# Chunked attention and two expert layers on one core: unread products placed by the planner, two weight loads under way, v in whole groups

## The chip, the cores and the metric

One core of a Trainium2 chip runs one program. The metric is the device time in microseconds (us) of one execution. TensorE is called PE, VectorE DVE, ScalarE ACT, GpSimd POOL, and SyncE SP; SP issues the DMA transfers.

## The reference

```python
for c in range(768 // 32):                     # chunks of 32 queries, 4 batches, 8 heads, 64 wide
    q_c = q[:, :, 32*c : 32*c + 32]
    keys = concat(mem_k, k[32*c - 16 : 32*c + 40])   # 8 memory keys, 16 to the left, 8 to the right
    a = softmax(q_c @ keys.T / 8)
    out[chunk] = a @ concat(mem_v, v[the same])
x = out as (3072 tokens, 512)
h = x @ w_in            # 512 x 2048
x = (h * clip(h + 3, 0, 6) / 6) @ w_out        # 2048 x 512
h = x @ moe2_w_in
y = max(0.01 * h, h) @ moe2_w_out
```

## The kernel before

The host only lays data out: q, k and v are cut into groups of 96 tokens and come as `raw`; the four weight matrices come as 64-bit numbers whose two halves the kernel joins to float32 (`decode`: one ACT instruction, L397, and four of DVE, L400, L404, L408 and L412). Every float32 operand of the layers is split into a high and a low part of type fp32r (a copy on ACT, L342, and a subtraction on DVE, L345), and a product of layers is three fp32r products: high with high, low with high, high with low.

The work on PE is the two layers, in blocks of 512 tokens; the attention is put between their products. The first block of tokens needs four pieces of attention before its first product: two units of 384 tokens (`unit`, one for each half of the heads; PSUM tiles `at` and `ab`) and two half units of 192 tokens (`half_unit` with `gp` 0, tiles `h` and `ac`). Then come two more half units (`gp` 1, tile `at`) and the units of the other tokens. A piece goes: scores on PE (L549, L816), maximum on DVE, exp on ACT (L573, L585, L842, L850), sum and norm on DVE (L603, L867), transposes on PE (L607, L871), a copy to SBUF on ACT (`take_p`), the product with v on PE (L627, L639, L887, L899), and the result into the operands `xh` (ACT) and `xl` (DVE). In front of the scores the keys are copied into windows (`windows`, on ACT, DVE or POOL).

The loads of v come in two layouts. "Whole" groups (`gp` 0: `whole = not gp`) take 128 rows per transfer, 4 transfers, and POOL copies the memory rows to their places (`memory`). The half units with `gp` 1 take 8 transfers instead, four of 56 partitions (L790) and four of 8 partitions (L792).

The order of all this is set by `schedule`. Each piece of work is a `Task` with a function that emits its instructions, a duration per engine, a key (its due place) and the buffers that it takes and uses. `schedule` simulates the five engines by these durations, the DMA queue by rates (`RATE...`) and constants, and the supply of PE's instructions by `feed` (`HELD`, `FETCHED`, `FETCH`), and at each free moment emits the task with the lowest key that is ready. The engines then run in exactly that order, each held only by semaphores. A task that was planned too early holds everything behind it on its engine.

Some products on PE are read by nobody: the identity with itself, written into a PSUM bank (`warm`, L466). The call `warm(n, after, home)` puts n of them behind a named task, by hand: 512 columns each into `ac` before and between the scores, 256 columns each into `ac` later on.

```python
    warm(2)
    warm(1, marks["s", 0, 0])
    warm(2, marks["s", 0, 1])
    warm(1, marks["s", 1, 0, 0])
    home = marks["b", 1, 1, 0][0]
    for m, n in ((("s", 1, 1, 0), 2), (("t", 0, 0), 3), (("t", 0, 1), 3), (("t", 1, 1, 0), 2), (("v", 1, 0, 0), 2)):
        warm(n, marks[m], home)
```

Of the kernel before, what the change touches and what calls it, by code (L numbers as in the profile page):

```python
# [23 lines left out]
QK = 2 * G + 2 * KW  # L24
# [33 lines left out]
RATE_QK, RATE, RATE_V, COLD = 380.0, 220.0, 300.0, 1.1  # L58
# [10 lines left out]
class Task:  # L69


    def __init__(self, fn, opts, key, after=(), allocs=(), uses=(), moe=False, issues=1, late=0, loads=False, ins=8):
        self.late, self.loads, self.ins = late, loads, ins
# [21 lines left out]
STARTS, LANDS, SURE = 1900.0, 500.0, 1500.0  # L95
HELD, FETCHED, FETCH, STALL = 447, 256, 5000.0, 250.0
# [7 lines left out]
def schedule(tasks, places, ends):  # L104
# [10 lines left out]
    queue = (0, HELD, None)  # L115
# [43 lines left out]
    def finish(task, e):  # L159
        for b in task.bufs:  # L160
# [17 lines left out]
    while events:  # L178
# [10 lines left out]
        while again:  # L189
            again = False  # L190
            for e, h in heaps.items():
# [44 lines left out]
                if e == "SP" or pick.loads:  # L236
                    at = now
                    for _ in range(pick.issues):
                        at = max(at, lanes[e].pop(0)) + ISSUE[e]
                        wire = max(wire, at + STARTS) + d / pick.issues  # L240
                        lanes[e].append(wire + LANDS)
                    free[e] = at if pick.loads else max(at, wire - QUEUED)
                    push(free[e], "free", None)
                    push(wire + LANDS + (SURE if pick.allocs else 0.0), "done", (pick, e))
# [12 lines left out]
def tile_attn_moe_moe2(ctx: ExitStack, tc: tile.TileContext, raw, w1i, w1o, w2i, w2o, out):  # L257
# [131 lines left out]
    def decode(src, f, key, early=None, after=(), place="wm", gate=(), late=0, own=True, split=None):  # L389
# [3 lines left out]
        def load(e):  # L393
            nc.sync.dma_start(out=make(t, ([128, 512, 2], U32)).rearrange("p w s -> p (w s)"), in_=src[f])
# [19 lines left out]
        k = add(load, {"SP": dma(524288, 380.0)}, key - 30 if early is None else early, after=after, allocs=[t])  # L414
# [31 lines left out]
    xbuf, xdone, turn, sent = {}, {}, [], {}  # L446

# [9 lines left out]
    marks = {}  # L457

    def warm(n, after=None, home=None):

        b, c = home or Buf("ac"), 2 if home else 4

        def fn(e):
            x = made(b)[:, 1, N - 128 * c:].rearrange("p (a n) -> p a n", a=c)
            for _ in range(n):
                nc.tensor.matmul(x, ident, ident.unsqueeze(1).to_broadcast([128, c, 128]), start=True, stop=True, skip_group_check=True)  # L466

        add(fn, {"PE": c * n * (220.0 if after else 430.0)}, after.key + 0.5 if after else -200.0, after=[after] if after else [], allocs=[] if home else [b], uses=[home] if home else [], ins=4 * n)

    def unit(j, quad, key, tag, own=False, direct=False, loads=None):  # L470
# [254 lines left out]
        t = marks["s", j, quad] = add(scores, {"PE": (COLD if direct else 1.0) * 1300.0}, key - 16, ins=192, after=t, allocs=[ps], uses=[*qk, *kw])  # L725
        scored = t
        if direct and quad in SHIFT:
            t = add(greatest, {"DVE": 2100.0}, key - 15, after=[t], allocs=[mx, e], uses=[ps])
            t = add(exp_all, {"ACT": act(2 * PAIRS * W)}, key - 13, after=[t], uses=[e])
            t = add(total, {"DVE": 1250.0}, key - 12, after=[t], allocs=[s], uses=[e])  # L730
        else:
# [4 lines left out]
            t = add(exp(1), {"ACT": 6 * 330.0}, key - 13, after=[t], uses=[ps, mx, e, s])  # L736
            t = add(total, {"DVE": 350.0}, key - 12, after=[t], uses=[s])
        t = add(norm, {"DVE": 900.0} if direct else {"POOL": 1800.0, "DVE": 900.0}, key - 11, after=[t], uses=[e, s])
        t = marks["t", j, quad] = add(transpose, {"PE": (COLD if direct else 1.0) * 600.0}, key - 7, ins=12, after=[t], uses=[e, ps])
        t = add(take_p, {"ACT": act(PAIRS * 128)}, key - 5, after=[t], uses=[pt, e])  # L740
# [950 lines left out]
```

## Time and profile before

| | |
|---|---|
| median of 3 runs (lowest, highest) | 1047.82 us (1047.02, 1048.76) |
| profiled execution | 1049.14 us, of which the span of instructions is 1047.40 |
| mean granted TensorE clock in it | 0.992 of full speed |
| PE busy | 1035.1 us, 99% of the span |
| DVE, ACT, POOL busy | 875.3, 693.7, 20.8 us |
| DMA | 220.49 MB, mean 211 GB/s |
| first product of the layers | 39.77 us after the span's start |

The profile's own time is that of a single execution; the median of the runs stands 1.32 us below it. Busy time of PE says that an instruction was in its pipeline, not that the array ran at full rate. A line such as L345 is that of a helper, so the tile names tell which work it is: `x4` counts records, and a float32 product on PE leaves two matmul records and two weight loads, a transpose one of each.

### The profile page before, as it was taken

The page shows a single profiled execution, that of the slowest core. Times are in us where ns is not written, and L with a number is a line of the kernel's source. Part 1 is how long each engine was busy: PE and PEld are TensorE (multiplying, and loading weights), DVE is VectorE, ACT ScalarE, POOL GpSimd, SP SyncE. Part 2 cuts the span into 40 slices and gives each one's busy share as a digit, 9 for nine tenths or more (in the row PEclk, how much of TensorE's full clock was granted, in tenths as well). Part 3 has the DMA queues.
Part 4 walks back from the last instruction along what each step waited for, and adds up shares of the span by engine and source line. Part 5 has one row for each costly group of instructions (what it writes and reads, how often), then busy time and mean ns, then how long its engine had stood idle before and what let it go on. Part 6 is the DMA issues. An engine that isn't in the chain of part 4 may idle for free.

```text
span 1047.4 us, 20225 instructions
## 1 busy us (share of the span) xinstructions
PE 1035.1 (99%) x7476; PEld 850.3 (81%) x7476; DVE 875.3 (84%) x1485; ACT 693.7 (66%) x1480; POOL 20.8 (2%) x30
## 2 busy tenths in 40 slices
PE   7999999999999999999999999999999999999998
PEld 4778988888788888888888888888888888888886
DVE  6898988778998778799999899999576998566775
ACT  4786876655888555476686576785565874666753
POOL 3010000000000000000000000000000000000000
PEclk8899999999999999999999999999999999999999
DMA  9889787876887979673648778546342454423451
GB/s 265 283 216 331 241 291 230 258 229 221 262 282 239 332 225 290 239 239 123 214 144 268 253 251 280 183 158 221 111 171 81 174 193 156 173 109 96 146 181 61
DMA packets 127314, 220.49 MB, mean 211 GB/s; under 512 B 12528, under 2 KB 76016, under 8 KB 127216
## 3 DMA queue, kind: packets, MB, share of 16 engines
q1 hardware_dynamic: 127216, 219.20, 63.9%
q8 instruction: 59, 0.97, 0.4%
q14 instruction: 39, 0.32, 0.1%
HBM read 156.24 MB, written 62.91 MB: 209 GB/s over the span
## 4 chain that ended last, share of the span: by engine, by line
PE 89%; DVE 4%; DMA 3%; ACT 3%; issue 1%; SPq 0%; DVEq 0%; ACTq 0%
PE y L1327 15%; PE y L1052 13%; PE y L1495 12%; PE h L1327 10%; PE h L1495 8%; PE hx L1495 8%; PE h L1003 7%; PE hx L1327 7%; PE h L1052 2%; PE at L639 2%; DMA w<-in_raw 2%; PE at L549 1%; DVE w L345 1%; PE at L607 1%; PE ac L466 1%
## 5 line engine op out<-in xcount | busy, mean ns | idle before, releaser
L345 DVE TENSOR_TENSOR w<-w 128x512 fp32r<-128x512 f32 (+2 forms) x393 | 322.9, 854 | 25.8 <-ACT w L342 23.9
L342 ACT CAST w<-w 128x512 fp32r<-128x512 f32 (+1 forms) x290 | 223.3, 803 | 13.4 <-PE hx L1495 3.6
L1052 PE MATMUL y<-g,w 128*128 128x512 f32 (+1 forms) x540 | 125.2, 375 | 0.9 <-ACT g L342 0.7
L1327 PE MATMUL y<-w 128*128 128x512 f32 x516 | 124.6, 390 | 0.0
L1327 PEld LDWEIGHTS y<-w 128*128 128x128 f32 x516 | 96.6, 188 | 20.1
L1052 PEld LDWEIGHTS y<-g,w 128*128 128x128 f32 x540 | 94.1, 189 | 19.0 <-ACT g L342 1.2
L342 ACT CAST g<-w 128x512 fp32r<-128x512 f32 x80 | 49.4, 620 | 63.8 <-PE y L1495 23.0
L1495 PE MATMUL y<-w 128*128 128x512 f32 x384 | 90.3, 389 | 0.0
L1495 PEld LDWEIGHTS y<-w 128*128 128x128 f32 x384 | 72.1, 188 | 14.9
L1301 ACT ACTIVATE w<-w 128x512 f32<-128x512 f32 x72 | 45.0, 630 | 40.4 <-DVE w L1372 18.1
L1003 PE MATMUL h<-xh,w 128*128 128x512 f32 (+1 forms) x288 | 66.1, 370 | 0.5 <-DVE w L345 0.5
L345 DVE TENSOR_TENSOR g<-w,g 128x512 fp32r<-128x512 f32 x80 | 54.1, 684 | 14.3 <-ACT g L342 14.2
L1495 PE MATMUL h<-w 128*128 128x512 f32 x264 | 62.1, 389 | 0.0
L1495 PE MATMUL hx<-w 128*128 128x512 f32 x252 | 59.2, 389 | 0.0
L1327 PE MATMUL h<-xl,w 128*128 128x512 f32 x240 | 58.3, 391 | 0.0
L1495 PEld LDWEIGHTS h<-w 128*128 128x128 f32 x264 | 49.6, 188 | 10.3
L1003 PEld LDWEIGHTS h<-xh,w 128*128 128x128 f32 x288 | 49.7, 189 | 9.9 <-DVE w L345 0.9
L1495 PEld LDWEIGHTS hx<-w 128*128 128x128 f32 x252 | 47.3, 188 | 9.8
L1327 PEld LDWEIGHTS h<-xl,w 128*128 128x128 f32 x240 | 44.8, 188 | 9.9 <-DVE xl L345 0.4
L1327 PE MATMUL y<-xh,w 128*128 128x512 f32 x216 | 52.2, 390 | 0.0
L1327 PEld LDWEIGHTS y<-xh,w 128*128 128x128 f32 x216 | 40.5, 188 | 8.4
L1052 PE MATMUL y<-w 128*128 128x512 f32 x180 | 46.6, 391 | 0.0
(244 smaller groups left out, 1852.2 us busy)
## 6 DMA issues: line engine op xcount, KB each, us to landing
w<-kept2i SPq DMA_DIRECT2D x42, 512.0 KB
w<-kept2o SPq DMA_DIRECT2D x42, 512.0 KB
w<-kept1i SPq DMA_DIRECT2D x28, 512.0 KB
a<-in_raw SPq DMA_DIRECT2D x20, 448.0 KB
w<-in_w1i SPq DMA_DIRECT2D x16, 512.0 KB
w<-in_w1o SPq DMA_DIRECT2D x16, 512.0 KB
w<-in_w2i SPq DMA_DIRECT2D x16, 512.0 KB
w<-in_w2o SPq DMA_DIRECT2D x16, 512.0 KB
```

Of the source, the lines that this page charges most:

```text
L342: nc.scalar.copy(out, in_) if e == "ACT" else engine(e).tensor_copy(out=out, in_=in_)
L345: engine(e).tensor_tensor(out=out, in0=a, in1=b, op=ALU.subtract)
L466: nc.tensor.matmul(x, ident, ident.unsqueeze(1).to_broadcast([128, c, 128]), start=True, stop=True, skip_group_check=True)
L549: nc.tensor.matmul(ps.t[h * CHUNK:(h + 1) * CHUNK, par, i * W:(i + 1) * W], qk[h // 2].t[r, gp, (h % 2) * G + c * CHUNK:(h % 2) * G + (c + ...
L607: nc.tensor.transpose(pt.t[:, i // NC, (i % NC) * 128:(i % NC + 1) * 128], pview()[:, i * 128:(i + 1) * 128], ident)
L639: nc.tensor.matmul(pv.t[(h % 2) * D:(h % 2 + 1) * D, par, (h // 2) * 2 * G + i * CHUNK:(h // 2) * 2 * G + (i + 1) * CHUNK], v[h // 2].t[r, ...
L1003: nc.tensor.matmul(h.t[:, o:o + n], w.t[:, 1 if p == 1 else 0, k * 128:(k + 1) * 128], x[:, k, c0:c0 + n], start=(p == 0 and k == 0 and o ...
L1052: nc.tensor.matmul(bank(banks[d])[:, c0:c0 + n], w.t[:, 1 if p == 1 else 0, d * 128:(d + 1) * 128], g.t[:, 1 if p == 2 else 0, at:at + n], ...
L1301: return add(lambda e: nc.scalar.activation(out=at(), in_=at(), func=AF.Prelu, alpha=0.01), {"ACT": act(N)}, key, after=[after], uses=uses)
L1327: nc.tensor.matmul(bank(to), wt(l, o)[:, kt * 128:(kt + 1) * 128].bitcast(F32R), operand(p, name, 1 if q == 2 else 0, kt).bitcast(F32R), s ...
L1495: nc.tensor.matmul(bank(to[d]), wt(1 if q == 1 else 0, o)[:, d * 128:(d + 1) * 128].bitcast(F32R), g.t[:, 1 if q == 2 else 0], start=(fres ...
```

## The change

Three things change in the code, and the planner's constants with them.

1. The calls of `warm` are gone. A task can open a PSUM bank (`opens`: its last reader is planned) and another closes it (`closes`: its next writer is planned). As long as no product of the layers has been placed, `schedule` fills each moment in which PE would have nothing with one unread product into an open bank: 64 columns at the start, 512 columns from 3500 ns of its own clock on.
2. `decode` gets `hold`: the weight loads 2 to 23, in the order in which they are declared, may be issued only when the load two places earlier has landed. A POOL instruction (`follow`) copies one number from that earlier load's buffer into the new one, and SP's transfer into the new buffer comes behind it.
3. The half units with `gp` 1 load v in whole groups too, with 4 transfers, `memory` on POOL, and the other order of scores and parts that goes with it: `xh` and `xl` of such a half unit come in 4 pieces.

```diff
-RATE_QK, RATE, RATE_V, COLD = 380.0, 220.0, 300.0, 1.1
+RATE_QK, RATE, RATE_V, COLD = 380.0, 220.0, 240.0, 1.1
...
-STARTS, LANDS, SURE = 1900.0, 500.0, 1500.0
-HELD, FETCHED, FETCH, STALL = 447, 256, 5000.0, 250.0
+STARTS, LANDS, SURE, SOONER, MOST = 1900.0, 250.0, (250.0, 1500.0), 20000.0, 8000.0
+HELD, FETCHED, ASKS, FETCH, STALL = 447, 256, 407, 2500.0, 250.0
+FIRST, LATER, FIRST_TILL = (64, 230.0), (512, 880.0), 3500.0
...
-            if comes is None and used >= held - FETCHED:
-                comes = at + FETCH
+            if comes is None and used >= held - ASKS:
+                comes = min(max(at, max((y for x, y in queued if x <= at), default=0.0)) + FETCH, at + MOST)
...
     def finish(task, e):
+        if task.opens:
+            spots.append(task.opens)
...
                 if pick is None:
+                    if e == "PE" and not progress and spots:
+                        cols, took = FIRST if now < FIRST_TILL else LATER
+                        filler(spots[0], cols)
+                        fill = Task(None, {"PE": took}, 0, ins=4)
+                        end, queue = feed(now, fill)
+                        free[e] = end
+                        push(end, "free", None)
                     continue
                 pick.taken = True
+                for b in pick.closes:
+                    if b in spots:
+                        spots.remove(b)
...
+        if hold:
+            before, landed = hold
+
+            def follow(e):
+                nc.gpsimd.tensor_copy(out=make(t, ([128, 512, 2], U32))[:1, 0, :1].bitcast(F32), in_=before.t[:1, 0, :1].bitcast(F32))
+
+            k = add(follow, {"POOL": 100.0}, early, after=[*after, landed], allocs=[t], uses=[before])
+            k = add(load, {"SP": dma(524288, 380.0)}, early, after=[k], uses=[t])
+        else:
+            k = add(load, {"SP": dma(524288, 380.0)}, key - 30 if early is None else early, after=after, allocs=[t])
+        arrivals.append((t, k))
...
+    def filler(b, cols):
+        t = made(b)
+        nc.tensor.matmul((t[:, 1] if b.tag[0] == "a" else t)[:, N - cols:], ident, ident.unsqueeze(1).to_broadcast([128, cols // 128, 128]) if cols > 128 else ident[:, :cols], start=True, stop=True, skip_group_check=True)
...
-        whole = not gp
+        whole = True
...
-    warm(2)
-    warm(1, marks["s", 0, 0])
...
+            parts = decode(..., hold=arrivals[i - 2] if 2 <= i < 24 else ())
```

What this does to the engines' orders is shown at three places. All instructions of the layers are the same in number; only their order differs.

PE, from the start to the scores of the second half unit (`ac`). The unread products are those with `ident` alone as input; `at` and `ab` are the units, `h` and `ac` the half units. Before:

```order
L466 MATMUL ac<-ident 128x512 x2
L549 MATMUL at<-w 32x64 x48
L466 MATMUL ac<-ident 128x512
L549 MATMUL ab<-w 32x64 x48
L466 MATMUL ac<-ident 128x512 x2
L816 MATMUL h<-w 32x64 x24
L466 MATMUL ac<-ident 128x512
L816 MATMUL ac<-w 32x64 x24
```

The same place now:

```order
L487 MATMUL ac<-ident 128x64 x16
L487 MATMUL ac<-ident 128x512 x4
L568 MATMUL at<-w 32x64 x48
L487 MATMUL ac<-ident 128x512
L568 MATMUL ab<-w 32x64 x48
L487 MATMUL ac<-ident 128x512 x3
L835 MATMUL h<-w 32x64 x24
L487 MATMUL ac<-ident 128x512
L626 MATMUL at<-ident,w 128x128 x6
L487 MATMUL ac<-ident 128x512
L835 MATMUL ac<-w 32x64 x24
```

Sixteen narrow and four wide unread products stand ahead of the first scores, where two wide ones stood, and the transposes of `at` come ahead of the scores of `ac`.

PE, from the product with v of the first unit (`at`) to the first product of the layers (`h<-xh,w`). Before:

```order
L627 MATMUL at<-w 64x32 x48
L607 MATMUL ab<-ident,w 128x128 x6
L466 MATMUL ac<-ident 128x256 x3
L871 MATMUL h<-ident,w 128x128 x3
L871 MATMUL ac<-ident,w 128x128 x3
L627 MATMUL ab<-w 64x32 x48
L466 MATMUL ac<-ident 128x256 x2
L887 MATMUL h<-w 64x32 x24
L466 MATMUL ac<-ident 128x256 x2
L887 MATMUL ac<-w 64x32 x24
L816 MATMUL at<-w 32x64 x24
L1003 MATMUL h<-xh,w 128x512 x8
```

The same place now:

```order
L646 MATMUL at<-w 64x32 x48
L626 MATMUL ab<-ident,w 128x128 x6
L890 MATMUL h<-ident,w 128x128 x3
L487 MATMUL h<-ident 128x512 x4
L646 MATMUL ab<-w 64x32 x48
L890 MATMUL ac<-ident,w 128x128 x3
L906 MATMUL h<-w 64x32 x24
L906 MATMUL ac<-w 64x32 x24
L835 MATMUL at<-w 32x64 x24
L1021 MATMUL h<-xh,w 128x512 x8
```

Nothing unread is written into `ac` any more after its scores, and nothing unread stands between the product with v of `ab` and the first product of the layers.

SP, from the second pair of weight loads (`in_w1i`, `in_w1o`) on; `L774` is q and k of a half unit with `gp` 1, `L790` and `L792` its v. Before:

```order
L394 DMA w<-in_w1i 128x1024
L394 DMA w<-in_w1o 128x1024
L394 DMA w<-in_w1i 128x1024
L394 DMA w<-in_w1o 128x1024
L774 DMA w<-in_raw 128x2x448
L790 DMA w<-in_raw 56x3x128
L792 DMA w<-in_raw 8x3x128
L790 DMA w<-in_raw 56x3x128
L792 DMA w<-in_raw 8x3x128
```

The same place now:

```order
L409 DMA w<-in_w1i 128x1024
L409 DMA w<-in_w1o 128x1024
L793 DMA w<-in_raw 128x2x448
L799 DMA w<-in_raw 128x2x128 x2
L802 DMA w<-in_raw 64x2x128 x2
L793 DMA w<-in_raw 128x2x448
L799 DMA w<-in_raw 128x2x128 x2
L802 DMA w<-in_raw 64x2x128 x2
L409 DMA w<-in_w1i 128x1024
L409 DMA w<-in_w1o 128x1024
```

Both of these half units are now loaded behind two weights instead of behind four, with 8 transfers for their v instead of 16, and the third pair of weights comes behind them.

On DVE the four decode instructions of the first weight now stand ahead of the norm of `ac`, and the norm of `at` ahead of the window copies of `ac`. On ACT the two window copies of the half units with `gp` 1 both stand ahead of the `xh` of `ac`; one did before.

## Rows read from the trace of the kernel before

**Rows 1.** The page: busy time of each engine and its share of the span.
```profile
PE 1035.1 (99%) x7476; PEld 850.3 (81%) x7476; DVE 875.3 (84%) x1485; ACT 693.7 (66%) x1480; POOL 20.8 (2%) x30
```
**Rows 2.** Stretches: us; busy us of PE, PEld, DVE, ACT, POOL; granted clock; DMA share; GB/s.
```profile
0.00:14.30 14.30, 10.85 (x221) 4.99 (x221) 7.18 (x21) 5.21 (x20) 4.30 (x15) 1.00 0.94 276
16.00:33.00 17.00, 14.99 (x175) 11.71 (x176) 11.98 (x30) 6.27 (x23) 6.02 (x8) 0.50 0.88 271
39.70:60.00 20.30, 19.13 (x185) 14.76 (x173) 19.86 (x49) 18.16 (x62) 0.00 (x0) 1.00 0.94 273
60.00:80.00 20.00, 19.44 (x219) 15.09 (x218) 19.36 (x38) 16.59 (x57) 2.79 (x2) 1.00 0.77 230
200.00:1044.00 844.00, 842.60 (x4527) 695.31 (x4525) 708.41 (x1126) 553.15 (x1009) 4.69 (x3) 1.00 0.60 198
```
**Rows 3.** Timeline of PE, 0 to 17: start, us, instructions, idle before and its releaser.
```profile
1.36 3.78 PE L466 MATMUL ac<-ident 128*128 128x512 f32 x4 [1.36 <-POOL three L308]
...
6.28 1.46 PE L549 MATMUL at<-w 64*32 64x64 f32 x92 [0.25 <-DVE w L342]
...
10.11 1.99 PE L466 MATMUL ac<-ident 128*128 128x512 f32 x4
...
14.37 0.45 PE L816 MATMUL h<-w 64*32 64x64 f32 x29 [1.40 <-issue]
14.75 1.13 PE L466 MATMUL ac<-ident 128*128 128x512 f32 x2
```
**Rows 4.** DMA queues, 11.5 to 12: the queue of PE's instructions; packets, MB, share.
```profile
q8 instruction: 1, 0.02, 16.6%
```
**Rows 5.** Timeline of PE, 17 to 40.
```profile
17.28 1.51 PE L607 MATMUL at<-ident,w 128*128 128x128 f32 x6
...
29.86 2.77 PE L466 MATMUL ac<-ident 128*128 128x256 f32 x6
...
33.46 1.78 PE L627 MATMUL ab<-w 64*64 64x32 f32 x96
...
39.77 2.17 PE L1003 MATMUL h<-xh,w 128*128 128x512 f32 x8
```
**Rows 6.** Timeline of DVE, 15 to 30.
```profile
15.51 0.77 DVE L342 COPY w<-w 128x336 f32<-128x336 f32 x4 [1.41 <-DMA w<-in_raw]
...
23.60 0.26 DVE L862 TENSOR_SCALAR mx<-mx 128x6 f32<-128x6 f32 x1 [1.62 <-ACT w L850]
...
29.72 1.15 DVE L345 TENSOR_TENSOR xl<-at,xh 128x256 fp32r<-128x256 f32 x4 [2.86 <-ACT xh L342]
```
**Rows 7.** Groups of DVE, 39.7 to 80: two of the four decode instructions; busy, mean ns.
```profile
L408 DVE SCALAR_TENSOR_TENSOR wm<-w,wm 128x512 uint32<-128x512 uint32 x5 | 3.4, 682 | 0.0
...
L400 DVE TENSOR_SCALAR wm<-wm 128x512 f32<-128x512 f32 x6 | 2.5, 418 | 0.0
```
**Rows 8.** Timeline of ACT, 21 to 40.
```profile
21.68 0.31 ACT L850 ACTIVATE w<-ac,mx 128x64 f32<-128x64 f32 x1 [2.00 <-PE ac L466]
...
33.66 0.49 ACT L342 COPY w<-ac 128x384 f32<-128x384 f32 x1
...
35.63 0.99 ACT L342 CAST xh<-ab 128x256 fp32r<-128x256 f32 x4
37.23 0.67 ACT L342 CAST xh<-h 128x128 fp32r<-128x128 f32 x4 [0.61 <-PE h L887]
37.75 1.14 ACT L342 COPY w<-w 128x336 f32<-128x336 f32 x4
39.23 0.62 ACT L342 CAST w<-wm 128x512 fp32r<-128x512 f32 x1 [0.34 <-DVE wm L408]
```
**Rows 9.** Timeline of SP's issues, 25 to 35.
```profile
25.19 0.49 SPq L790 DMA_DIRECT2D w<-in_raw  x1
...
34.15 0.41 SPq L774 DMA_DIRECT2D w<-in_raw  x1
```
**Rows 10.** Chain of waits, 60 to 80: a load of q and k.
```profile
71.52 4.75 DMA a<-in_raw
```

More of the change, by code (lines that the diff above doesn't have):

```diff
@@ L69, with __init__ @@
 class Task:
-    def __init__(self, fn, opts, key, after=(), allocs=(), uses=(), moe=False, issues=1, late=0, loads=False, ins=8):
-        self.late, self.loads, self.ins = late, loads, ins
+    def __init__(self, fn, opts, key, after=(), allocs=(), uses=(), moe=False, issues=1, late=0, loads=False, ins=8, opens=None, closes=()):
+        self.late, self.loads, self.ins, self.opens, self.closes = late, loads, ins, opens, closes
         self.fn, self.opts, self.key, self.moe, self.issues = fn, opts, key, moe, issues
@@ L114, in schedule @@
     lanes = {e: [0.0] * LANES for e in ISSUE}
-    queue = (0, HELD, None)
+    queue, queued = (0, HELD, None), []
     def feed(at, task):
@@ L387, in tile_attn_moe_moe2, with decode @@
     wbuf, wtask = {}, {}
-    def decode(src, f, key, early=None, after=(), place="wm", gate=(), late=0, own=True, split=None):
+    def decode(src, f, key, early=None, after=(), place="wm", gate=(), late=0, own=True, split=None, hold=()):
         t, m = Buf("w"), Buf(place)
         def load(e):
-            nc.sync.dma_start(out=make(t, ([128, 512, 2], U32)).rearrange("p w s -> p (w s)"), in_=src[f])
+            nc.sync.dma_start(out=made_as(t, [128, 512, 2], U32).rearrange("p w s -> p (w s)"), in_=src[f])
         def absolute(e):
@@ L455, in made @@
         return b.t if b.t is not None else make(b)
[L457 to L468, printed above, removed]
+    begun_at = Buf("ac")
+    def filler(b, cols):
+        t = made(b)
+        nc.tensor.matmul((t[:, 1] if b.tag[0] == "a" else t)[:, N - cols:], ident, ident.unsqueeze(1).to_broadcast([128, cols // 128, 128]) if cols > 128 else ident[:, :cols], start=True, stop=True, skip_group_check=True)
     def unit(j, quad, key, tag, own=False, direct=False, loads=None):
@@ L724, in unit @@
             l2 = [add(memory(i), {"POOL": 1500.0}, key - 20, after=[l2[i]], uses=[v[i]]) for i in range(2)]
-        t = marks["s", j, quad] = add(scores, {"PE": (COLD if direct else 1.0) * 1300.0}, key - 16, ins=192, after=t, allocs=[ps], uses=[*qk, *kw])
+        t = add(scores, {"PE": (COLD if direct else 1.0) * 1300.0}, key - 16, ins=192, after=t, allocs=[ps], uses=[*qk, *kw])
         scored = t
         if direct and quad in SHIFT:
-            t = add(greatest, {"DVE": 2100.0}, key - 15, after=[t], allocs=[mx, e], uses=[ps])
+            t = add(greatest, {"DVE": 2100.0}, key - 15, after=[t], allocs=[mx, e], uses=[ps], opens=ps)
             t = add(exp_all, {"ACT": act(2 * PAIRS * W)}, key - 13, after=[t], uses=[e])
@@ L965, in half_unit @@
         t = add(norm, {"DVE": 500.0}, key - 11, after=[t], uses=[e, s])
-        t = marks["t", j, quad, gp] = add(transpose, {"PE": cold * 300.0}, key - 7, ins=6, after=[t], uses=[e, *banks])
-        t = add(take_p, {"ACT": act(NC * 128)}, key - 5, after=[t], uses=[*banks, e])
-        t = marks["v", j, quad, gp] = add(values_whole if whole else values, {"PE": cold * 900.0}, key, ins=96, after=[t, l2], uses=[e, v, *banks])
+        t = add(transpose, {"PE": cold * 300.0}, key - 7, ins=6, after=[t], uses=[e, *banks], closes=banks[:1])
+        t = add(take_p, {"ACT": act(NC * 128)}, key - 5, after=[t], uses=[*banks, e], opens=banks[0])
+        t = add(values_whole if whole else values, {"PE": cold * 900.0}, key, ins=96, after=[t, l2], uses=[e, v, *banks], closes=banks)
         jb, at = divmod(begins, N)
@@ L1588, in tile_attn_moe_moe2 @@
             alone_ = f >= KF // 2
-            parts = decode(src, f, at - 8, early[i] if i < len(early) else min(at - 38, 6 * i - 40), splits[before:before + 1] if before >= 0 else (), "ys" if i % 2 else ("wm", "st")[f // 2 % 2] if alone_ else "wm", gate=behind if 3 <= i < 6 else (), own=alone_, split=which if alone_ else None)
+            parts = decode(src, f, at - 8, early[i] if i < len(early) else min(at - 38, 6 * i - 40), splits[before:before + 1] if before >= 0 else (), "ys" if i % 2 else ("wm", "st")[f // 2 % 2] if alone_ else "wm", gate=behind if 3 <= i < 6 else (), own=alone_, split=which if alone_ else None, hold=arrivals[i - 2] if 2 <= i < 24 else ())
             if alone_:
@@ L1639, in tile_attn_moe_moe2 @@
         constants()
-        schedule(tasks, places, ends)
+        schedule(tasks, places, ends, filler, [begun_at])
 def kernel(**inputs):
```

34 lines of the change are left out of this document (15 added, 19 removed).

## The prediction

> **What bounds the kernel now.** I read the page's busy times first, then a table of stretches, then the timelines of PE, DVE, ACT and SP over the first 40 us, where the change is. PE is busy for 99% of the span [rows 1], and from 200 to 1044 us for 842.6 of 844 us at the full clock [rows 2]. The change leaves every product of the layers in place, so behind the first product (39.77 us, [rows 5]; 1047.40 - 39.77 = 1007.6 us of span) it can only add or remove waits. There is little to remove there. What it can win lies in the opening, and three things in it are slow:
>
> - From 16 to 33 us the granted clock is 0.50 of full speed, that is 1.2 of 2.4 GHz, though PE counts as busy for 14.99 of 17 us [rows 2]. A wide unread product (512 columns) costs 3.78 / 2 = 1.89 us at the very start, and at the full rate 1.99 - 1.13 = 0.86 us, the difference between two of them and one [rows 3]. The clock fell behind a stretch in which PE had no wide products and sat idle for 1.40 us [rows 3], and was up again soon after the run of unread products at 29.86 [rows 5].
> - Unread products go into `ac` between its scores and its exp: ACT waits 2.00 us for them [rows 8], and DVE then 1.62 us for ACT [rows 6].
> - The v of the half units with `gp` 1 goes out in pieces: SP is at it from 25.19 until the next q and k at 34.15 [rows 9].
>
> Behind the first product DVE bounds as much as PE for a while: 19.86 + 19.36 = 39.2 us busy of 40.3 between 39.7 and 80 [rows 2]. A first product that comes earlier pays only if DVE has done more by then. It can: in the opening it idles 1.62 and 2.86 us for ACT [rows 6], and decode steps can go there.
>
> **The change part by part.**
>
> *Start of PE.* Sixteen narrow and four wide unread products replace two wide ones. A narrow one has no row. Unread products cost in proportion to their columns (256 columns at half clock: 2.77 / 3 = 0.92 us [rows 5], half of 1.89), which gives 1.89 / 8 = 0.24 us at the low end. At the high end it is bound by its two weight loads of 128 columns: a transpose with one such load takes 1.51 / 6 = 0.25 us at half clock [rows 5], so 0.50. I take 0.24, because the two widths that have rows scale. Then the narrow ones end at 1.36 + 3.8 = 5.2 us and the wide ones at 5.2 + 4 x 0.86 = 8.6; the high end, at half clock throughout, is 1.36 + 8.0 + 4 x 1.89 = 16.9. Scores of `at` start at 8.6 instead of 6.28 and take 1.46. That puts DVE's first maximum some 1 us later, and DVE waits 1.41 us before its window copy at 15.51 [rows 6]; the norm of `at` now stands in that gap. Cost behind it: 0.2 us. If that cover is gone, 1 us.
>
> *PE's instructions.* The wait of 1.40 us for "issue" [rows 3] comes with a fetch on the queue of instructions between 11.5 and 12 [rows 4]. Up to its end PE has run 221 matmul records (x221 in the stretch 0 to 14.3 [rows 2]). Now 40 records (the unread ones) + 96 + 2 come before the scores of `ab`, so the 221st lies in those, which would run from 11.0 to 12.5. If the code comes as now, at 14.37, they and all that hangs on them are 2 us later; if it comes with PE's earlier use, nothing is lost. I take 0.5, nearer the low end because more records are used early, and again 0.5 for the later fetches, which now meet a PE that runs twice as fast.
> The Trainium skill's page "Runtime: NRT & Kernel Launch", section "Instruction fetch mechanics", says that crossing such a block is mostly hidden and that PE's store holds 2048 instructions. The row of the wait disagrees for this opening; by the page both terms would be 0 and the forecast 1 us lower.
>
> *DVE and ACT from 16 to 26 us.* The waits of 2.00 and 1.62 us go, since nothing is written into `ac` between scores and exp. What is late next is DVE: four decode instructions, 2 x 0.42 + 2 x 0.68 = 2.2 us [rows 7], now stand ahead of the norm of `ac`. Against the 1.62 us saved, that norm ends 0.6 us later than now. Nobody waits for it: it is needed only behind the product with v of `ab`.
>
> *From `ab` to the first product.* With the full clock and the four wide products behind the transposes of `h` (about 22.8 + 3.4 = 26.2), the product with v of `ab` takes its 1.78 us [rows 5] and ends at 28.0, not at 35.2. Then ACT decides by its new order: `xh` of `ab` 0.99, the copy of `ac` 0.49, two casts 1.24, window copies 1.14, `xh` of `h` 0.67, window copies 1.14, `xh` of `ac` 0.67 [rows 8], together 6.3 us, so 34.3. With the other 0.5 us for code the first product stands at 34.8: **5.0 us earlier** than 39.77. The window copies need q and k by about 31; these now go out behind the second pair of weights and not at 34.15 [rows 9], and cost nothing as long as that holds.
>
> *Whole groups.* `xh` and `xl` of two half units come in four pieces. Four pieces take 0.67 us on ACT [rows 8]; one piece can save no more than that, so 0 to 1.3 us in the stretch that DVE bounds. I take 0.4. The `memory` copies go to POOL, which does nothing from 39.7 to 60 [rows 2].
>
> *Two loads under way.* Each hold is one tiny POOL copy; SP's queue waits behind it, and raw loads and stores stand behind SP. From 39.7 to 80 DVE decodes 5 loads through `wm` [rows 7] and, by the group beside it, as many through `ys`: one load per 4.0 us, a pair per 8.1. A load took 4.75 us [rows 10]; with some 1 us for POOL and SP (an estimate: SP's issues take 0.4 to 0.5 us [rows 9], the copy no more) a pair can be renewed every 5.8 us. I cost it at nothing. The bounds are 0 and what the second rival below gives.
> The page "DMA: Bandwidth & Descriptors", section "Rules for kernel authors", of the Trainium skill speaks against this part: issue a DMA early and wait late, so that its fixed cost overlaps. By that rule the rival of late weights is what happens; the row of 4.75 us leaves room instead.
>
> **Sum.** -5.0 + 0.4 = -4.6 us. Against the profiled execution that is a span of 1047.4 - 4.6 = 1042.8 and a run of 1044.5. That execution stands 1.3 us above the median shown, so I forecast a median of 1047.8 - 4.6 = **1043.2 us**. A measurement of this kernel can tell about 0.2% from no change, 2.1 us, so "faster" means below 1045.7 and "slower" above 1049.9.
>
> **The rivals.**
>
> 1. *The half clock comes back just before the first product.* From 26.2 to 34.8 nothing unread is left, PE does small products for about 5 us and waits for ACT. For it: the fall at 16 came behind such a stretch [rows 2, 3]. Against it: the small products between 33.5 and 39.8 kept the full clock, though with unread ones between. The layers' products would run for 3 to 5 us at half rate, which loses 1.5 to 2.5 us: 1044.7 to 1045.7, say 1045.2.
> 2. *Weights late, the case on the slower side.* If a held pair takes 8.5 us to land behind raw loads and stores, plus 1 us of hand-over, each of five pairs between 35 and 80 is 1.4 us late, and DVE has no slack there to hide it: 7 - 4.6 = +2.4, 1050.2 us. It decides from a landing time of about 7 us, and beats the gain from 8.
> 3. *A dear start.* With the high end of 16.9 for the scores of `at`, 8.3 us late, the first product comes at about 43: 1051. It turns the gain into a loss once those scores start later than 8.6 + 5.0 = 13.6.
> 4. *Code waits of 2 to 3 us* instead of 1: 1044.7 to 1045.7, or a little above.
> 5. *It does not do what it says*: loads set the opening (DMA is 0.88 busy from 16 to 33 [rows 2]), so PE gets the full clock and waits instead; less than 1 us is won, 1047.
>
> **How the numbers follow.** Forecast 0.45, half clock 0.18, late weights 0.10, dear start 0.07, code 0.10, no effect 0.10. Faster: 0.45, most of the half clock (0.13) and some of the code case (0.04), 0.62. Slower: the second and third rival, 0.17. The rest, 0.21, is within 0.2%. The range reaches below the forecast by what the unknown terms allow (no code waits, pieces free, and one us more where DVE's idle time goes), to 1040.5, and above to the first, fourth and fifth rivals, 1048.5; the slower two are left out.
>
> **What would show it.** Right: granted clock 1.00 in every stretch between 8 and 40 us; first product between 34 and 36; ACT's wait of 2.00 before the exp of `ac` gone; PE and DVE between 35 and 80 no idler than now. Wrong: clock 0.50 anywhere after 20; the scores of `at` later than 10; a wait of PE or DVE on decoded weights; SP waiting on POOL for several us, with raw loads behind it.

## The result, and the profile after

| | before | changed |
|---|---|---|
| median (lowest, highest) | 1047.82 us (1047.02, 1048.76) | 1058.03 us (1056.20, 1058.91), 5 runs |
| ratio to before, 95% interval | | 1.0094 (1.008 to 1.0108) |
| profiled execution, its span | 1049.14, 1047.40 us | 1057.12, 1055.3 us |
| first product of the layers | 39.77 us (35.66 in a second profile, below) | 43.16 us |
| rest of the span | 1007.6 us (1009.3) | 1012.1 us |

The change is **0.94% slower**, 10 us, where 4.6 us less were forecast. The same stretches of the changed kernel, in the columns of [rows 2]:

```profile
0.00:14.30 14.30, 12.95 (x137) 9.83 (x137) 2.31 (x12) 2.59 (x6) 4.30 (x15) 1.00 0.95 278
16.00:33.00 17.00, 13.59 (x276) 7.71 (x258) 12.82 (x29) 9.40 (x45) 7.15 (x14) 0.90 0.99 280
39.70:60.00 20.30, 18.93 (x255) 15.04 (x255) 17.03 (x47) 16.98 (x66) 1.94 (x5) 0.83 1.01 254
60.00:80.00 20.00, 19.92 (x221) 15.51 (x221) 19.86 (x45) 18.64 (x63) 4.38 (x7) 1.00 0.87 304
200.00:1044.00 844.00, 841.56 (x4525) 694.59 (x4524) 715.69 (x1137) 554.49 (x1009) 7.46 (x4) 1.00 0.60 199
```

The clock from 16 to 33 is up from 0.50 to 0.90, near the forecast (a second profile of before, below, has 0.93 there without the change), but in the first 14.3 us PE has run 137 matmul records where it had run 221: it spent the time on unread products. From 39.7 to 60 the clock is now 0.83. PE's timeline, which answers to [rows 3, 5]:

```profile
13.20 1.17 PE L568 MATMUL at<-w 64*32 64x64 f32 x96
...
15.35 1.05 PE L568 MATMUL ab<-w 64*32 64x64 f32 x83
19.75 0.34 PE L568 MATMUL ab<-w 64*32 64x64 f32 x13 [3.35 <-issue]
...
35.74 1.78 PE L646 MATMUL ab<-w 64*64 64x32 f32 x96
...
37.92 0.95 PE L906 MATMUL h<-w 64*64 64x32 f32 x40
40.64 0.30 PE L906 MATMUL h<-w 64*64 64x32 f32 x5 [1.77 <-issue]
...
43.16 3.75 PE L1021 MATMUL h<-xh,w 128*128 128x512 f32 x8 [0.43 <-ACT xh L357]
46.70 1.91 PE L1021 MATMUL h<-xl,w 128*128 128x512 f32 x4
48.41 2.08 PE L1021 MATMUL h<-xh,w 128*128 128x512 f32 x8
```

The scores of `at` start at 13.20 (before, 92 of their 96 records ran from 6.28), and two waits for code ("issue") follow, 3.35 and 1.77 us, where the first profile of before had one of 1.40 and the second three, 1.56, 0.86 and 0.19. The first eight products take 3.75 us (2.17 before), at the half clock (the granted clock is 0.50 from 44.0 to 48.4). The groups of the same engine up to 14 us, with the shapes kept apart (busy us, mean ns of a record; an unread product leaves two records):

```profile
L487 PE MATMUL ac<-ident 128*128 128x64 f32 x32 | 7.1, 423 | 1.4 <-POOL three L323 1.4
L487 PE MATMUL ac<-ident 128*128 128x512 f32 x8 | 5.0, 788 | 0.0
```

So a narrow unread product cost 7.1 / 16 = 0.44 us and a wide one 5.0 / 4 = 1.25. The wide ones changed rate on the way: their records took 1.10 us in the mean between 8.2 and 10.8 us, as at the very start of the kernel before (3.78 us for four records that overlap, [rows 3]), and 0.60 from 11.3 on. The column of the granted clock reads 1.00 for the whole stretch and does not show this. The fetch of code came between 17 and 17.5 us, not at 11.5 as in [rows 4]:

```profile
q8 instruction: 1, 0.02, 16.2%
```

### The profile page after: what moved, and what is told of

Read it like the earlier page. It is cut to its first block, busy times and chain, and to the rows that moved or that the text cites. A ratio compares the mean times of both kernels' runs of the same rounds, so it can differ in the third digit from the quotient of the medians.

```text
span 1055.3 us, 20351 instructions
## 1 busy us (share of the span) xinstructions
PE 1039.7 (99%) x7502; PEld 853.2 (81%) x7502; DVE 880.1 (83%) x1492; ACT 693.9 (66%) x1483; POOL 37.0 (4%) x58
## 4 chain that ended last, share of the span: by engine, by line
PE 90%; DVE 5%; ACT 2%; issue 1%; DMA 1%; POOL 0%; SPq 0%; DVEq 0%; ACTq 0%; POOLq 0%
PE y L1070 14%; PE y L1345 13%; PE y L1513 12%; PE h L1345 9%; PE h L1021 8%; PE h L1513 8%; PE hx L1345 8%; PE hx L1513 8%; PE h L1070 2%; PE ac L487 2%; PE at L658 2%; DVE w L360 1%; PE at L568 1%; ACT w L357 1%; DVE w L1373 1%
## 5 line engine op out<-in xcount | busy, mean ns | idle before, releaser
L1345 PE MATMUL y<-w 128*128 128x512 f32 x516 | 124.2, 390 | 0.0
L1513 PE MATMUL y<-w 128*128 128x512 f32 x384 | 90.3, 389 | 0.0
L1021 PE MATMUL h<-xh,w 128*128 128x512 f32 (+1 forms) x288 | 69.4, 380 | 2.8 <-issue 1.7
L1513 PEld LDWEIGHTS h<-w 128*128 128x128 f32 x264 | 49.5, 188 | 10.3
L1390 DVE TENSOR_TENSOR w<-y,w 128x512 f32<-128x512 f32 x35 | 23.9, 687 | 32.4 <-PE y L1345 26.1
```

What stands on the lines that cost most here:

```text
L1021: nc.tensor.matmul(h.t[:, o:o + n], w.t[:, 1 if p == 1 else 0, k * 128:(k + 1) * 128], x[:, k, c0:c0 + n], start=(p == 0 and k == 0 and o ...
L1345: nc.tensor.matmul(bank(to), wt(l, o)[:, kt * 128:(kt + 1) * 128].bitcast(F32R), operand(p, name, 1 if q == 2 else 0, kt).bitcast(F32R), s ...
L1390: done[2] = add(lambda e: nc.vector.tensor_tensor(out=half_of(x, 0), in0=bank(bb), in1=ut.t[:, 0], op=ALU.add), low, key, after=[k, done[1 ...
L1513: nc.tensor.matmul(bank(to[d]), wt(1 if q == 1 else 0, o)[:, d * 128:(d + 1) * 128].bitcast(F32R), g.t[:, 1 if q == 2 else 0], start=(fres ...
```

## The experiments

**The base itself, and three changes that mean nothing.** These came last, but the rest is read more easily after them. `before_again` is the kernel before, unchanged.

> The kernel before, unchanged, for a second profile of it. In b_stir1 and b_stir3 its order of the opening ran at the full clock and the first product stood at 35.7 and 36.2. If the half clock from 16 to 33 in the first profile belongs to that one execution and not to the order: granted clock 1.00 there, first product at 35.5 to 36.5, span 1044 to 1046.5. If it belongs to the order: 0.50 there again, first product at 39 to 40.5.

Measured: 1047.48 us, ratio 1.0005 (0.9991 to 1.002), span 1045.0. Its stretch from 16 to 33 and its timeline of PE:

```profile
16.00:33.00 17.00, 14.11 (x329) 11.46 (x329) 15.96 (x38) 9.86 (x34) 5.89 (x8) 0.93 0.88 269
```

```profile
29.55 1.10 PE L627 MATMUL ab<-w 64*64 64x32 f32 x51 [0.86 <-issue]
...
35.66 2.11 PE L1003 MATMUL h<-xh,w 128*128 128x512 f32 x8
...
38.51 1.98 PE L1003 MATMUL h<-xh,w 128*128 128x512 f32 x8
```

The half clock of [rows 2] belonged to that one execution: `b_stir1` and `b_stir3` below, which have the same opening, show 1.00 in that stretch. With the clock at 0.93 the same order reaches the first product at 35.66, 4.1 us earlier. That is most of the 5.0 us that the prediction meant to win. The span is shorter by less, 1047.4 - 1045.0 = 2.4 us. Of the 88 runs of before that the experiments were compared with, the 14 with a mean granted clock of 0.993 or less (the profiled one had 0.992) average 1049.6 us and the 49 with 0.997 or more 1047.5.

`b_stir1` and `b_stir3` alter a constant of the planner by 1%, so that the order is another from about 102 us on in the first and from about 73 in the second, by the traces of ACT and DVE; `a_stir1` does it to the changed kernel, where two neighbours on ACT change places at 39.8 us already and DVE's order differs from about 154.

```diff
-RATE_QK, RATE, RATE_V, COLD = 380.0, 220.0, 300.0, 1.1
+RATE_QK, RATE, RATE_V, COLD = 384.0, 220.0, 300.0, 1.1
...
-STARTS, LANDS, SURE = 1900.0, 500.0, 1500.0
+STARTS, LANDS, SURE = 1920.0, 500.0, 1500.0
```

> The kernel before with one rate of the planner changed by 1% (384 for 380 at q and k), a change that means nothing: the order stays that of before up to about 110 us and differs behind. Theory H (the parts of the change cost by what they do): within 1.5 us of before. Rival T (the order of before is one chosen among many, and any other order costs some us by its own waits): 2 us or more slower, by idle time of PE behind 100.

> The kernel before with the planner's start time of a transfer at 1920 instead of 1900, another change that means nothing: the order differs from about 90 us on. Theory H: within 1.5 us of before. Rival T: 2 us or more slower, by idle time of PE behind 90.

> The changed kernel with the same meaningless 1% on the rate of q and k: the order differs from about 130 us on. Theory H: within 1.5 us of the changed kernel's 1058.0. Rival T (where the order of the changed kernel is no chosen one, another is as likely better as worse): off by 1.5 to 4 us to either side.

Measured: 1046.72 us (ratio 0.9991, 0.9982 to 1.0001), 1048.19 (1.0002, 0.9992 to 1.0012), and 1056.59 (1.0088, 1.0074 to 1.0102). Another order behind the opening costs nothing here, so rival T falls for that part of the run. A meaningless change of the order within the first 70 us was not tried.

**Front and hold taken out, the order kept.** The products and copies are planned as in the change but not issued; nothing that is read is left out. `a_front` drops the first 18 unread products (16 narrow, 2 wide), `a_nohold` the POOL copies of the hold, `a_front_nohold` both, and `a_front_tail` drops the 18 and adds a wide one ahead of the last two products with v.

```diff
     def filler(b, cols):
         t = made(b)
+        if len(dropped) < 18:
+            dropped.append(cols)
+            return
...
             def follow(e):
-                nc.gpsimd.tensor_copy(...)
+                return
...
         def values_whole(eng):
+            if not gp:
+                filler(banks[0], 512)
```

> The changed kernel with its order untouched, but the first eighteen unread products (sixteen narrow, two wide) not issued, so that two wide ones stand ahead of the first scores as before the change. Theory A (the dear start: scores of at at 13.2 us instead of 6.3, and a code wait of 3.4 us that comes later with it): scores of at near 6.5 us, first product 5 to 6 us earlier than 43.2, so near 37.5, median near 1052.5. Rival B (held weight loads): the first product may move, but the decode behind it waits for weights, so the median stays above 1055.5. Rival C (the new order itself is worse behind the first product): like A in the opening, and the rest of the span stays near 1012 us, 4.5 us above the 1007.6 of the kernel before.

> The changed kernel with its order untouched, but the tiny POOL copies that hold each early weight load until the load two places earlier has landed are not issued. Theory A: within 1.5 us of 1058.0, since the opening is set by the start of PE. Rival B: 4 us or more faster, 1054 or less, and the loads go out earlier between 35 and 100 us. If the hold helps (instructions of PE fetched sooner), it gets slower by 1 to 3 us and the code waits of PE grow.

> Both edits together: two wide unread products in front, and no hold. Theory A: within 1.5 us of the run with the front alone. Rival B: 4 us or more below it, and at or below the kernel before, 1047.8.

> As the run with the short front, plus one wide unread product ahead of the product with v of h and one ahead of that of ac, where the changed kernel has none. If the half clock after the opening (0.50 from 41.9 us in the changed kernel, first eight records of the layers 3.75 us instead of 2.1) comes from PE's small products and waits there, the clock stays at 1.00 and the median falls by 1 to 2 us against the short front alone; two wide ones cost 1.7 us of PE, which is hidden as long as ACT decides the first product. If not, it is 0 to 2 us slower.

Measured: 1055.51, 1055.96, 1056.26 and 1056.26 us (ratios 1.0075, 1.0075, 1.0073, 1.0079, each within 0.0025 either way). The first product came at 36.54 in `a_front`, 6.6 us earlier than in the change, yet only 2.5 us came off the time: the rest of the span grew from 1012.1 to 1053.7 - 36.54 = 1017.2 us, which none of the three expectations had. The copies by themselves are worth 2.1 us with the long front (`a_nohold`; between the two expectations), and nothing with the short one. The wide products of `a_front_tail` did not bring the clock back: its first eight products still take 3.26 us, and it is no faster than `a_front`. So something behind the first product takes the rest. As the copies are gone in `a_front_nohold` and the order is the same, it is put down to the order; that is an argument, and the next runs plan other orders.

**The parts alone, on the kernel before.**

```diff
-        whole = not gp
+        whole = True
```

(`b_whole`, which also has the planner's lower rate for q and k of the half units with `gp` 0; `b_const` has the constants and the supply rule of the change, `b_hold` its `decode` with `hold`, `b_fill_short` the placing of unread products by `schedule`, with two wide ones ahead of the first scores.)

> The kernel before with v of the late half units in whole groups alone (and the planner's lower rate for their q and k); the order of the loads stays that of before. Theory A: the pieces cost what the prediction put on them, 0 to 1.3 us, median within 2 us of before. Rival B: idle time of PE between 80 and 400 of 2 us and more, as in all kernels of the change so far, median 1050 to 1053.

> The kernel before with the planner's new constants alone (rate of v, landing times, supply of PE's instructions); the four weights in a row stay. Theory A: the constants reorder little that is waited for, median within 2 us of before, and PE is idle for less than 1 us between 80 and 400. Rival C (the constants bring the idle time that all kernels of the change show between 80 and 400): 2 to 3 us of idle time there, median 1049.5 to 1052.

> The kernel before with the hold alone: one weight load, then q, k and v of a half unit, then two weights and so on, where four weights went out in a row. Theory A: PE waits for decoded weights between 40 and 80 for 3 to 6 us, median 1051 to 1055. Rival B: less than 1 us of such waits, median within 2 us of before.

> The kernel before with the placing of unread products by the planner alone (two wide ones at the start, none written into a bank whose scores are waited for), old constants, v of the late half units in pieces, no hold. If the opening is what such placing wins, as the prediction had it: first product at 35 to 37 and median 1043 to 1046. If the decoded weights set the pace up to 80 in any case: the same first product, waits for weights of 2 us and more between 45 and 80, and a median within 2 us of before.

| | median | ratio, 95% | first product |
|---|---|---|---|
| `b_whole` | 1049.54 us | 1.0019 (1.0009 to 1.003) | 35.72 us |
| `b_const` | 1050.74 | 1.0023 (1.001 to 1.0036) | 35.52 |
| `b_hold` | 1058.39 | 1.0094 (1.0078 to 1.011) | 37.84 |
| `b_fill_short` | 1053.76 | 1.0057 (1.0042 to 1.0071) | 36.27 |

The hold alone, costed at nothing, loses as much as the whole change. ACT waits 7.1 us for weights in it between 36 and 80 us, in five waits, where `before_again` has 2.8 in two; that is the way of theory A, past its 1055. None of the parts gains, and none brings the first product clearly ahead of 35.66. `b_whole` came within theory A's 2 us. `b_const` came as its rival C said: PE idles 320 - 317.1 = 2.9 us between 80 and 400. `b_fill_short` met neither of its two expectations.

**The same parts, with the planner told.** `a_short` has two wide unread products at the start, and the planner knows it; `a_short_unheld` has no hold either, so that the planner places the loads anew; `a_unheld` has the long front without the hold. `as_unheld` drops the 18 products behind the planner's back, `a_short_unheld_feed` goes back to the old supply rule, `a_narrow_unheld` has 12 narrow products for the two wide ones.

```diff
-                    if e == "PE" and not progress and spots:
-                        cols, took = FIRST if now < FIRST_TILL else LATER
+                    if e == "PE" and not progress and spots and (begun or fills < 2):
+                        cols, took = LATER if begun else (512, 1890.0)
+                        fills += 1
...
-            parts = decode(..., hold=arrivals[i - 2] if 2 <= i < 24 else ())
+            parts = decode(...)
```

> The changed kernel without its first 18 unread products, and without the hold in the declaration of the weight loads, so that the planner may place the loads anew: four weights in a row go out ahead of the two raw loads of the late half units, where two did. Theory A (the hold as a rule of the plan sets the order of the loads, and the order makes weights late behind an early first product): first product at 36 to 38, no wait of PE for decoded weights over 1 us between 40 and 80, median 1047 to 1050. Rival B (whole groups, or the planner's other constants, set what is lost behind the first product): waits for weights of 3 us or more in that stretch again, median 1054 to 1056.

> The changed kernel with two wide unread products ahead of the first scores, and the planner told so (in the earlier run the 18 products were dropped behind the planner's back, which also shifted its count of PE's instructions). The hold stays. Theory H (the hold's order of loads costs time behind an early first product): first product at 35 to 38, PE waits for decoded weights 2 to 5 us between 45 and 110, median 1053 to 1057. Rival M (the earlier runs lost time because the planner's count was wrong): code waits below 2 us in all, no long waits for weights, median 1047 to 1050.

> The kernel of the run before it in this list, without the hold, the planner free to place the loads: four weights in a row go out ahead of the raw loads. Theory H: 4 us or more faster than with the hold, median 1047 to 1051. Rival S (the new rule for the supply of PE's instructions makes waits for code in any order): waits of PE for issue of 4 us and more in all, median 1053 to 1057.

> As the one before it, with the planner's old rule for the supply of PE's instructions (the next block is asked for when all but 256 are used, and comes 5 us later). Rival S: waits for issue fall below 3 us in all, and the time by what they fall, 3 to 6 us. Theory H: the rule changes little, under 2 us either way, median 1046 to 1051.

> The changed kernel with its long front of unread products, without the hold, the planner free to place the loads. It fills the fourth cell beside the changed kernel (long front, hold; 1058.0), the short front with hold (1055.9) and the short front without (1049.8). Theory H (the hold's order costs about 6 us in either front): 1051 to 1053.5. Rival D (the long front lets the weights come in time whatever the order, so that there the hold costs little): 1055 to 1058.

> The changed kernel without the hold and with 12 narrow unread products at the start in place of 16 narrow and 4 wide ones (the short front had 2 wide). Twelve narrow ones take about as long as two wide ones (12 x 0.31 = 3.7 us) and use 40 of PE's instructions more, so blocks of code should be asked for earlier. If the supply of code holds the first product at 36: the wait for code ahead of the last products with v falls from 4.0 to 3.0 to 3.5 us, first product at 35 to 36, median 1046.5 to 1049.5. If the scores of the first unit are held by PE's work at the half clock: they end later than with two wide ones, first product at 37 or later, median 1050 to 1053.

Medians in us, with the first product in the profile:

| | hold | no hold |
|---|---|---|
| long front | 1058.03 (43.16) | 1057.09, `a_unheld` (44.07) |
| short front | 1055.86, `a_short` (36.34) | 1049.83, `a_short_unheld` (36.12) |

This table is the best answer that the runs give. Hold and long front each cost 6 to 7 us where the other is absent (1055.86 - 1049.83 = 6.0; 1057.09 - 1049.83 = 7.3), and together hardly more than one of them (8.2). They act as two bounds side by side, not as two terms of a sum: behind a late first product the held weights come in time (in the changed kernel no engine waits for a weight between 36 and 80 us), behind an early one they don't. So rival D was right of the hold in the changed kernel, and theory H with the short front. One thing keeps it from being a proof. Each kernel here is planned anew, and three others with a short front and no hold, reported below, lie at 1050.1, 1053.2 and 1057.0: the order that the planner finds is worth up to 7 us, as much as either part. That the hold costs time behind an early first product has a second witness in `b_hold`; the 7.3 us of the long front have none.

How the hold delays is seen in `a_short` (SP's issues of two weights, ACT, PE):

```profile
47.75 0.35 SPq L412 DMA_DIRECT2D w<-in_w1i  x1
...
55.72 0.35 SPq L412 DMA_DIRECT2D w<-in_w1i  x1
```

```profile
53.27 0.68 ACT L415 ACTIVATE wm<-w 128x512 f32<-128x512 f32 x1 [3.02 <-DMA w<-in_w1i]
...
61.48 0.66 ACT L415 ACTIVATE wm<-w 128x512 f32<-128x512 f32 x1 [2.15 <-DMA w<-in_w1i]
62.04 0.64 ACT L415 ACTIVATE ys<-w 128x512 f32<-128x512 f32 x1
62.59 0.60 ACT L360 CAST g<-r 128x512 fp32r<-128x512 f32 x1
```

```profile
63.24 3.34 PE L1073 MATMUL y<-g,w 128*128 128x512 f32 x7 [3.62 <-ACT g L360]
```

A weight issued at 47.75 is there for ACT at 53.27, one issued at 55.72 at 61.48: 5.5 to 5.8 us. The two issues stand 8.0 us apart; from 36 to 80 us SP's weight loads waited 5.1 us for raw loads to land and 2.9 for the copies of the hold, so it is more the order than the copies. ACT runs in order and stands before the late weight, with the cast of `g` behind it, and PE waits 3.62 us for that cast. The waits of ACT from 36 to 80 us (us in total, times, longest), in `a_short` and then in `a_short_unheld`:

```profile
ACT wm L415 <- DMA w<-in_w1i: 8.8, 5, 3.0
ACT ys L415 <- DMA w<-in_w1o: 2.0, 2, 1.6
```

```profile
ACT ys L415 <- DMA w<-in_w1o: 0.5, 1, 0.5
```

By 43 us eleven weights have been issued without the hold, seven with it, and twelve in `before_again`. That lead is not enough by itself: `b_fill_short`, `as_unheld` and `a_short_unheld_feed` have eleven as well. (The profiled run of `a_short` was the slowest of five, that of `a_short_unheld`, 1046.42, the fastest of eleven; the medians decide.) The Trainium skill's rule to issue a DMA early and wait late ("DMA: Bandwidth & Descriptors", "Rules for kernel authors"), which the prediction set aside, agrees with these rows.

The products of the layers that PE has issued by a given time show where a lead is lost (one for each record of 512 columns, a half for 256, from the groups by shape in windows from 0):

| by (us) | 50 | 60 | 80 | 160 |
|---|---|---|---|---|
| `before_again` | 47 | 85 | 148 | 412 |
| `before`, first profile | 31 | 70 | 140 | 404 |
| changed | 19 | 52 | 125 | 385 |
| `a_unheld` | 17 | 46 | 120 | 388 |
| `a_short` | 40 | 72 | 128 | 372 |
| `a_short_unheld` | 48 | 84 | 147 | 412 |
| `a_short_unheld_feed` | 50 | 85 | 139 | 395 |
| `b_hold` | 42 | 80 | 125 | 377 |

The first profile of before is 16 behind its second at 50 and 8 at 80: half of that late start is made up. With the long front 28 to 30 are missing at 50 and 24 to 27 still at 160 us. `a_short` is 7 behind at 50, 20 at 80 and 40 at 160: half of its loss comes behind the stretch shown above, and what makes that half was not taken apart.

The other three kernels without the hold. `as_unheld`: 1057.03 us (1.009, 1.0072 to 1.0109), 7.2 us slower than `a_short_unheld`, of which it differs by the planner not knowing what was dropped; its waits for code are

```profile
PE at L573 <- issue: 5.2, 3, 3.1
PE ac L911 <- issue: 2.7, 1, 2.7
PE at L651 <- issue: 1.5, 1, 1.5
```

9.4 us where `a_short_unheld` has one of 4.0; the 5.2 of the first row lie behind 80 us. `a_short_unheld_feed`: 1053.21 (1.0053, 1.0039 to 1.0067), with the same wait of 4.1:

```profile
32.05 0.88 PE L909 MATMUL ac<-w 64*64 64x32 f32 x18 [4.07 <-issue]
32.86 3.78 PE L1024 MATMUL h<-xh,w 128*128 128x512 f32 x8
```

The old rule does not remove the wait, so rival S falls; theory H's "under 2 us either way" fails too, by 3.4 us. And this kernel has the earliest first product of all, 32.86, 3.3 us ahead of `a_short_unheld`: it leads by two products at 50 us and is 17 behind at 160. `a_narrow_unheld`: 1050.09 (1.0017, 1.0007 to 1.0027), with the first product at 37.06, as its second alternative had it; the code wait fell from 4.0 to 3.7 only, and the narrow products ended at 6.7, not at 5.1:

```profile
1.36 5.39 PE L490 MATMUL ac<-ident 128*128 128x64 f32 x24 [1.36 <-POOL three L326]
6.67 1.62 PE L571 MATMUL at<-w 64*32 64x64 f32 x96
...
32.60 1.46 PE L909 MATMUL ac<-w 64*64 64x32 f32 x38 [3.72 <-issue]
```

Twelve took 5.39 us, 0.45 each; the 0.31 us in the expectation was read off a timeline row that joins narrow and wide products.

No kernel beat the one before. Open is why the placing by the planner alone (`b_fill_short`) costs 6.0 us when the same placing with the new constants and whole groups (`a_short_unheld`) costs 2.3.

## Why the prediction was wrong

**The base.** "From 16 to 33 us the granted clock is 0.50" was read as a property of the order. `before_again` shows that it is one of the execution. The first product stands at 35.66 with the clock at 0.93, so the forecast of 34.8 left 0.9 us to win, not 5.0. The first profile's own time, 1.32 us above the median, had been noted and set aside. This step alone turns the forecast into "no change".

**The first product taken for the span.** The prediction said that an earlier first product "pays only if DVE has done more by then", and then put all of the 5.0 us into the sum. Between the two profiles of before 4.1 us at the first product are worth 2.4 of span; 6.6 us are worth 2.5 in `a_front`; and `a_short_unheld_feed` is 3.3 us earlier than `a_short_unheld` and 3.4 slower. So even with the base as it was read, the gain would have been smaller. The steps that follow bear on the loss.

**Start of PE: mis-sized.** A narrow unread product was taken at 0.24 us, with 0.50 for the other bound; it measured 0.44, near the bound by weight loads. The wide ones cost 1.25, not 0.86: the full rate was forecast, and the first of them ran at the rate of the start (1.10 us a record against 0.60). Scores of `at`: 8.6 forecast, 13.20 measured, 4.6 us later. "Cost in proportion to their columns" holds between 512 and 256 columns and failed at 64; the transpose was the nearer row.

**PE's instructions: mis-sized.** 0.5 + 0.5 us were taken, 3.35 + 1.77 came ahead of the first product, 4.1 more. The 221st record lay where the prediction put it (40 + 96 + 2 + 83 records ahead of the wait in `ab`). The block came neither at 14.37 nor without loss, but 2.3 to 2.8 us behind a fetch that stood 5.5 us later than before; PE had used its instructions later, which would explain the fetch but was not tested. The Trainium skill's "mostly hidden" ("Runtime: NRT & Kernel Launch", "Instruction fetch mechanics") fits the run as a whole, where PE waits for issue five times in the changed kernel with 59 packets on that queue, but not the opening.

```profile
q8 instruction: 59, 0.97, 0.4%
```

The two terms together, 4.6 + 4.1 = 8.7 us, give the first product at 34.8 + 8.7 = 43.5; it came at 43.16. That this closes is in part luck. The product with v of `ab` ends at 35.74 + 1.78 = 37.5 where 28.0 was forecast, 9.5 us late; the start (4.6) and the first wait (3.35 - 0.5 = 2.85) give 7.5 of these, and 2.0 stay unexplained. (The 22.8 us from which the prediction went on there is not worked out in it.) From `ab` on, the first product took 5.6 us instead of 6.8, with the second wait in it. And `a_nohold`, whose two waits are 2.19 and 0.27 us, has its first product at 42.84, only 0.3 earlier.

**DVE and ACT from 16 to 26 us.** The wait of ACT for the unread products [rows 8] is gone, as said; it saved nothing, since the scores come late; at 21.61 us ACT waits 4.16 for DVE's maximum of `ab`:

```profile
21.61 0.31 ACT L604 ACTIVATE w<-ab,mx 128x64 f32<-128x64 f32 x1 [4.16 <-DVE mx L589]
```

**Two loads at a time: costed at nothing, wrong in general.** In the changed kernel itself the hold costs little: 0.9 us against `a_unheld`, 2.1 against `a_nohold`, about what the runs can tell. With the first product near where the prediction put it, it would have cost some 6 us, by `a_short` against `a_short_unheld`. The step compared a renewal of 5.8 us with a need of one pair per 8.1. A load by itself took 5.5 to 5.8 us, a pair in `a_short` was renewed after 8.0, and the need was averaged over a stretch for which the kernel before had already issued eleven or twelve weights ahead. The hold took that lead away.

**Whole groups.** 0.4 us, bound 1.3; `b_whole` measured 2.0 (0.9 to 3.1 by its interval). **Constants:** no term at all; `b_const` measured 2.4 us (1.0 to 3.8). The two were measured on the kernel before, and need not add up in the changed one.

**The rivals.** The dear start comes nearest, but not by its own condition: it asked for the scores of `at` at 16.9 and named 13.6 as the turning point, and they came at 13.20. That the first product came at its "about 43" all the same took more waits for code than the fourth rival's, 5.1 us; the agreement is luck in part. Its price, 1051, was too low by the wrong base: 43.16 - 35.66 = 7.5 us, not 3.4. The half clock of the first rival came as well: twelve products take 48.41 - 43.16 = 5.25 us, 38.51 - 35.66 = 2.85 in `before_again`, so 2.4. The rest of the span differs by 0.4, and together these are 1055.3 - 1045.0 = 10.3. The sum says where the changed kernel is late, not what taking a part away would win: `a_front` takes back 6.6 us of it and wins 2.5. Late weights are real, but in `a_short` and `b_hold`, not here.

## What to carry to other kernels

Before a stall in a profile becomes a gain to win, see whether a second execution of the same kernel has it: clock and spans of the runs tell (here 0.992 against 0.998). Where two things bound side by side, take each out alone and both together; one experiment that removes one of them finds little either way (2 us of the front's 7), and the other then looks innocent. A lead of loads built up early is not seen in an average rate: count what has been issued by the time that the consumer starts. And an earlier start of the main work is not a shorter run: see what has been done at several later times before it goes into a sum.

## What the hardware showed unexpectedly

Sixteen unread products of 64 columns cost 7.1 us, 0.44 each, where a wide one at the very start of the kernel before cost 1.89 [rows 3]: about a quarter of the price for an eighth of the columns. The prediction's high end, two weight loads of 128 columns, fits better than the columns do; the loads were not measured by themselves.

In all thirteen kernels with the planner's unread products the first eight products of the layers run wholly or in part at the half clock (2.96 to 3.78 us), in `b_const` too (3.78), behind a stretch of small products and waits, for code or, in `b_const`, of 1.92 us for ACT. The kernel before (2.17 and 2.11 us in its two profiles), `b_whole` and `b_hold` (2.11) keep the full clock there, with unread products between the last products with v; but `b_const` and `a_front_tail` have those as well, so they alone do not explain it.
